# A first sequence in feed-forward units of 128, 256 and 384 tokens in place of three of 256, with a new order of all instructions

## The chip, the core and the metric

The kernel runs on one core of a Trainium2 chip. A core has TensorE (PE in the profile, its weight loads PEld), VectorE (DVE), ScalarE (ACT), GpSimd (POOL) and SyncE (SP), which issues the transfers here. The metric is the device time of one execution in microseconds, and less is better. Times of a comparison are medians of runs on one chip.

## What is computed

Four sequences of 768 tokens go through a linear attention with 8 heads of 48 channels, whose state decays by a complex factor, and then through a feed-forward layer with a short convolution and a gate:

```python
for t in range(S):                     # per sequence and head
    S_re, S_im = ar*S_re - ai*S_im + k[t] v[t]^T, ar*S_im + ai*S_re
    y[t] = q[t] S_re
h = relu(x @ w_in)                     # x: y with heads side by side, 384 channels; w_in 384x1024
conv = sum_k conv_w[k] * h[t + k - 1]  # 3 taps over tokens, zero outside the sequence
out = (h * sigmoid(conv)) @ w_out      # 1024x384
```

## The kernel before

**Attention.** The 24 chunks of 128 tokens (6 for each sequence) are worked through in 12 segments of two. For each segment `a_pre`, `a_log`, `a_trig`, `c_pre` and `c_exp` turn the decay into running logs and angles on ScalarE and VectorE (lines 479 to 577). `c_post` (579) forms the products `qkc_t` (L592), writes them to DRAM (L596) and reads them back in another layout as `stk` (L598). For each chunk `c_chunk` (604) transposes keys on TensorE (L612), copies them (L613), adds to the state (L619) and copies the state (L626). `attention` (656) computes scores (`scores`, L652), multiplies them by a mask on VectorE (L667) in two halves, and multiplies with the values and the state (L676). The result of a chunk is rounded on ScalarE to the high part of `x` (L702), and VectorE makes the low part of it (L703). These two are called the x copy of a chunk here.

**Feed-forward.** It runs over units, each a run of tokens of one sequence (`UNITS`, line 34). A unit's x tiles hold its tokens and one more at each side, since the convolution reaches over the edge. That neighbour column comes out of another unit's x tile by small copies (`halo`, 710, L395). So a unit can start when the chunk behind its last token has its x copy:

```python
UNITS = [[256] * 3, [384] * 2, [384] * 2, [256] * 3]
def need(u):
    b, t0, n = units[u]
    return b * NC + min((t0 + n) // C, NC - 1)
```

A unit takes four steps of two 128-channel blocks each. The front of a step (`moe_front`, 746) is 2 x 9 first-layer matmuls of n + 2 columns into `h_ps` (L758; operands in the type float32r, split in a high and a low part, three products for each of three blocks of channels), the relu on ScalarE (L762) and two passes of the convolution on VectorE (L763, L765). The back (`moe_back`, 768) is the gate's tanh on ScalarE (L420), a product on VectorE (L777), the split of the result into high and low (L783 on ScalarE, L786 on VectorE), and second-layer matmuls of 384 columns into `o` (L793), 2 x 3 for each 128 tokens. After the last step the sums leave by ScalarE (L800) and a transfer (L803). There are two buffers of each x tile and of `h_ps`.

**Order.** The order of the instructions on each engine is written out in a table, `ORDER` (lines 108 to 226): numbers of groups, in program order, for PE, DVE, ACT, POOL and SP. `in_order` (256) chains each engine's instructions in that order and sets ScalarE's table loads (L272) where the next function isn't in the loaded table. So each engine works strictly through its list, and an instruction that waits holds up all that stand behind it on that engine. The weights are loaded and split in the first 80 us, mixed with the rest (L348 to L351, L387 to L390).

Of the kernel before, what the change touches and what calls it, by code (L numbers as in the profile page):

```python
# [33 lines left out]
UNITS = [[256] * 3, [384] * 2, [384] * 2, [256] * 3]  # L34
# [128 lines left out]
    "DVE": [105, 24, 106, 111, 57, 112, 107, 63, 58, 59, 28, 113, 69, 29, 70, 109, 71, 60, 64, 65, 117, 46, 66, 72,  # L163
# [117 lines left out]
def linear_attention_moe_kernel(ctx: ExitStack, tc: tile.TileContext, a, at0, qk, v, w_in, conv_w, w_out, out):  # L281
# [453 lines left out]
    mst = {}  # L735
    units = [(b, sum(UNITS[b][:i]), n) for b in range(B) for i, n in enumerate(UNITS[b])]
    nu = len(units)
# [339 lines left out]
```

## Time and profile before

| | before |
|---|---|
| median of 3 runs | 386.64 us (384.75 to 387.11) |
| profiled execution | 385.09 us, its span 383.3 |
| TensorE busy | 345.3 us, 90% |
| TensorE weight loads busy | 323.5 us, 84% |
| VectorE busy | 337.3 us, 88% |
| ScalarE busy | 333.1 us, 87% |
| mean granted TensorE clock | 0.971 |

The span runs from the first to the last instruction. Busy shares are means over stages with different limits, so the tables by stage say more than the shares. A matmul's length in the trace holds its latency; what it costs in a stream is the distance from its start to the next one's.

### The profile page before, as it was taken

To read this page: it belongs to the slowest core of one execution; us is meant where nothing else is said; L and a number is where in the kernel's file an instruction comes from. 1 tells how busy PE (TensorE), PEld (TensorE's weight loads), DVE (VectorE), ACT (ScalarE), POOL (GpSimd) and SP (SyncE) were. 2 spreads that over 40 slices of the span, in tenths; PEclk is the share of its full clock that TensorE was granted. 3 is DMA by queue.
4 is the path that set the end of the run, shared out by engine and by line. 5 is a ranking of instruction groups with operands and counts; after the bars stand their busy time and mean duration, and the time that the engine had idled before them with its cause. 6 is when DMAs were issued, how large, how long until landed. Compare 5 with 4: busy or idle time off the path is not lost.

```text
span 383.3 us, 12048 instructions
## 1 busy us (share of the span) xinstructions
PE 345.3 (90%) x5220; PEld 323.5 (84%) x5220; DVE 337.3 (88%) x552; ACT 333.1 (87%) x566; POOL 6.9 (2%) x42
## 2 busy tenths in 40 slices
PE   2577277899999999999999999999999999999993
PEld 1566275789999999999998998999999899999993
DVE  3999999989999989999999989898999988567680
ACT  5999999989999999999999998999999965346561
POOL 5000000000000000000000000000000000000000
PEclk9989758999999999999999999999999999999999
DMA  7999989995894957975959566974849828101011
GB/s 285 346 365 345 246 290 254 313 225 198 316 265 165 271 132 292 280 210 235 250 170 289 120 234 264 218 236 167 213 146 301 284 109 213 53 3 65 1 44 50
DMA packets 33423, 81.12 MB, mean 212 GB/s; under 512 B 2128, under 2 KB 23632, under 8 KB 31824
## 3 DMA queue, kind: packets, MB, share of 16 engines
q1 hardware_dynamic: 33360, 80.25, 68.4%
q8 instruction: 43, 0.70, 0.8%
q14 instruction: 20, 0.16, 0.1%
HBM read 56.65 MB, written 23.59 MB: 209 GB/s over the span
## 4 chain that ended last, share of the span: by engine, by line
PE 83%; ACT 7%; DVE 6%; issue 1%; DMA 1%; DVEq 0%
PE h_ps L758 27%; PE o L793 27%; PE ps L676 10%; PE ps L652 9%; PE s_ps L619 4%; PE ps L612 3%; PE o L471 2%; ACT w_t L420 2%; ACT L272 1%; ACT x_t L420 1%; DMA a_t<-in_at 1%; DVE qkc_t L592 1%; ACT w_t L484 1%; DVE p_t L667 1%; DVE x_t L497 0%
## 5 line engine op out<-in xcount | busy, mean ns | idle before, releaser
L793 PE MATMUL o<-wo,hg 128*128 128x384 f32 x576 | 122.3, 342 | 0.5 <-issue 0.4
L758 PE MATMUL h_ps<-x,wi 128*128 128x258 f32 (+1 forms) x720 | 122.4, 308 | 0.0
L758 PEld LDWEIGHTS h_ps<-x,wi 128*128 128x128 f32 x720 | 109.2, 189 | 1.1 <-ACT h_t L762 0.3
L793 PEld LDWEIGHTS o<-wo,hg 128*128 128x128 f32 x576 | 98.6, 188 | 3.1 <-issue 1.1
L272 ACT ACT_TABLE_LOAD x41 | 52.6, 1283 | 0.7
L652 PE MATMUL ps<-stk 96*64 96x128 f32 (+1 forms) x768 | 39.8, 257 | 9.9 <-DMA stk<-qkd 8.2
L652 PEld LDWEIGHTS ps<-stk 96*64 96x64 f32 x768 | 36.0, 142 | 14.8 <-ACT kn L613 10.8
L420 ACT ACTIVATE g_t<-g_t,cw 128x256 f32<-128x256 f32 (+1 forms) x80 | 42.5, 550 | 5.1 <-DVE g_t L765 4.9
L763 DVE SCALAR_TENSOR_TENSOR g_t<-h_t,cw 128x256 f32<-128x256 f32 (+1 forms) x80 | 41.6, 532 | 5.1 <-ACT h_t L762 4.9
L762 ACT ACTIVATE h_t<-h_ps 128x258 f32<-128x258 f32 (+1 forms) x80 | 33.5, 426 | 13.4 <-PE h_ps L758 13.1
L765 DVE SCALAR_TENSOR_TENSOR g_t<-h_t,cw,g_t 128x256 f32<-128x256 f32 (+1 forms) x80 | 41.8, 533 | 1.1
L592 DVE TENSOR_TENSOR qkc_t<-w_t,zz_t 128x1536 f32<-128x1536 f32 x24 | 41.7, 1751 | 0.3
L777 DVE SCALAR_TENSOR_TENSOR g_t<-g_t,h_t 128x512 f32<-128x512 f32 (+1 forms) x40 | 31.6, 791 | 5.7 <-ACT g_t L420 5.6
L786 DVE TENSOR_TENSOR hg<-g_t,hg 128x512 fp32r<-128x512 f32 (+1 forms) x40 | 31.6, 791 | 2.5 <-ACT hg L783 2.4
L783 ACT ACTIVATE hg<-g_t 128x512 fp32r<-128x512 f32 (+1 forms) x40 | 28.5, 716 | 5.9 <-DVE g_t L777 5.5
L667 DVE TENSOR_TENSOR p_t<-ps,mask 128x384 f32<-128x384 f32 x48 | 26.1, 552 | 7.4 <-PE ps L652 6.3
L676 PE MATMUL ps<-p_t,v_t 128*32 128x64 f32 x1344 | 25.7, 223 | 2.6 <-issue 1.7
L676 PEld LDWEIGHTS ps<-p_t,v_t 128*32 128x32 f32 x1344 | 23.0, 112 | 3.7 <-issue 2.2
L676 PE MATMUL ps<-stk,s_sb 96*32 96x128 f32 x640 | 22.1, 275 | 0.6 <-issue 0.4
L612 PE MATMUL ps<-ident,qkc_t 128*128 128x128 f32 x120 | 20.2, 289 | 1.4 <-DMA stk<-qkd 1.1
L484 ACT ACTIVATE w_t<-a_t 128x1536 f32<-128x1536 f32 x12 | 17.9, 1489 | 3.9 <-DMA a_t<-in_at 3.9
L577 DVE TENSOR_TENSOR w_t<-w_t,qk_t 128x1536 f32<-128x1536 f32 x12 | 21.0, 1752 | 0.0
(100 smaller groups left out, 450.8 us busy)
## 6 DMA issues: line engine op xcount, KB each, us to landing
qkd<-qkc_t SPq DMA_DIRECT2D x24, 768.0 KB, 4.2
stk<-qkd SPq DMA_DIRECT2D x24, 768.0 KB, 7.6
v_t<-in_v SPq DMA_DIRECT2D x12, 1024.0 KB, 8.7
qk_t<-in_qk SPq DMA_DIRECT2D x12, 768.0 KB, 6.0
a_t<-in_a SPq DMA_DIRECT2D x10, 768.0 KB, 5.1
out<-os_t SPq DMA_DIRECT2D x24, 192.0 KB, 4.5
hg<-in_w_out SPq DMA_DIRECT2D x8, 384.0 KB, 5.4
h_t<-in_w_in SPq DMA_DIRECT2D x8, 384.0 KB, 4.9
```

The costliest lines, as they stand in the source:

```text
L272: row = [nc.scalar.preload_act_table_set(sets[k]).ins] + row
L420: nc.scalar.activation(out, in_, func=func, **kw)
L592: nc.vector.tensor_tensor(out=qkc, in0=e[:, q:q + 1].broadcast_to([128, 2, NG * w]), in1=zz, op=ALU.mult)
L612: nc.tensor.transpose(tr[:, g - lo], kv[:, g // NG, g % NG], ident)
L652: nc.tensor.matmul(o, lhsT=kt[:, 2 * i + u, part * HC + r:part * HC + r + TM], rhs=qt[:, 2 * i + u, part * HC:C], start=first, stop=part = ...
L676: nc.tensor.matmul(yp[r0:r0 + 32, q // 4, cols], lhsT=left, rhs=right, start=r0 not in started, stop=stop, tile_position=(0, r0), skip_gro ...
L758: nc.tensor.matmul(hp, lhsT=wi[iw][:, f, kt], rhs=x[ix][:, kt], start=(k == 0), stop=(k == 8))
L762: nc.scalar.activation(h, hp, func=AF.Relu)
L763: nc.vector.scalar_tensor_tensor(out=g, in0=h[:, 0:n], scalar=cw[:, f, 0:1], in1=h[:, 1:n + 1], op0=ALU.mult, op1=ALU.add)
L765: nc.vector.scalar_tensor_tensor(out=g, in0=h[:, 2:n + 2], scalar=cw[:, f, 2:3], in1=g, op0=ALU.mult, op1=ALU.add)
L777: nc.vector.scalar_tensor_tensor(out=g, in0=g, scalar=1.0, in1=h[:, :, 1:n + 1], op0=ALU.add, op1=ALU.mult)
L793: nc.tensor.matmul(ops[t][:min(C, n - t * C)], lhsT=hg[:, k, t * C:min((t + 1) * C, n)], rhs=w[:, fw], start=(f == 0 and i == 0), stop=(f ...
```

## The change

The first sequence is cut into units of 128, 256 and 384 tokens. Unit 0 needs chunks 0 and 1 then (before: 0 to 2), unit 1 chunks up to 3 (before: 4), and unit 2 up to 5 as before. The widths of all tiles of these units follow. The other three sequences keep their units. The order of the groups is listed anew for all five engines, with as many groups on each engine as before.

```diff
-UNITS = [[256] * 3, [384] * 2, [384] * 2, [256] * 3]
+UNITS = [[128, 256, 384], [384] * 2, [384] * 2, [256] * 3]
 ORDER = {
-    "PE": [31, 35, 32, 33, 36, 34, 153, 207, 208, 209, 210, 211, 212, 222, 169, 171, 223, 224, 225, 175, 226, 227,
+    "PE": [31, 35, 36, 32, 33, 34, 153, 287, 288, 283, 284, 285, 286, 169, 171, 298, 299, 300, 302, 303, 301, 175,
...
```

What the numbers move is seen in the instructions themselves. On TensorE, behind the last products of chunk 1 (`ps<-p_t,v_t`), there stood before:

```order
L676 MATMUL ps<-stk,s_sb_117 32x128 x16
L612 MATMUL ps<-ident,qkc_t 128x128 x4
L676 MATMUL ps<-p_t,v_t 32x64 x28
L612 MATMUL ps<-ident,qkc_t 128x128 x2
L619 MATMUL s_ps<-v_t,kn 32x48 x24
L612 MATMUL ps<-ident,qkc_t 128x128 x6
L652 MATMUL ps<-stk 64x128
```

And now, with `x_473` and `x_474` the high and low part of unit 0's x:

```order
L676 MATMUL ps<-stk,s_sb_117 32x128 x16
L676 MATMUL ps<-p_t,v_t 32x64 x28
L612 MATMUL ps<-ident,qkc_t 128x128 x6
L758 MATMUL h_ps<-x_473,wi_131 128x130
L758 MATMUL h_ps<-x_474,wi_131 128x130
L758 MATMUL h_ps<-x_473,wi_131 128x130
L758 MATMUL h_ps<-x_474,wi_131 128x130
L758 MATMUL h_ps<-x_473,wi_132 128x130 x2
```

First-layer matmuls begin here, where before the scores of chunk 2 came next; before, the first of them (of 258 columns) stood behind the scores of chunk 3. All 72 of unit 0 stand between this place and the next one.

On TensorE, around the last products of chunk 3, before:

```order
L676 MATMUL ps<-stk,s_sb_119 32x128 x16
L676 MATMUL ps<-p_t,v_t 32x64 x28
L758 MATMUL h_ps<-x_473,wi_131 128x258
L758 MATMUL h_ps<-x_474,wi_131 128x258
L758 MATMUL h_ps<-x_473,wi_132 128x258
```

And now, with `x_546` the x of unit 1:

```order
L676 MATMUL ps<-stk,s_sb_119 32x128 x16
L676 MATMUL ps<-p_t,v_t 32x64 x28
L793 MATMUL o_1228<-wo_133,hg_1232 128x384
L793 MATMUL o_1228<-wo_134,hg_1232 128x384
L612 MATMUL ps<-ident,qkc_t 128x128 x4
L793 MATMUL o_1228<-wo_133,hg_1233 128x384
L793 MATMUL o_1228<-wo_133,hg_1232 128x384
L793 MATMUL o_1228<-wo_134,hg_1232 128x384
L793 MATMUL o_1228<-wo_133,hg_1233 128x384
L612 MATMUL ps<-ident,qkc_t 128x128 x2
L758 MATMUL h_ps<-x_546,wi_131 128x258
L758 MATMUL h_ps<-x_547,wi_131 128x258
```

Before, unit 0 was still in its first layer here (18 of 72 matmuls done). Now its second layer has begun, and the next first-layer matmuls are those of unit 1.

On VectorE, from the second mask product of chunk 2 to that of chunk 3, before (the weights' split, L348 to L390, and the segment steps L485, L546 and L553 are mixed in):

```order
L546 SCALAR_TENSOR_TENSOR zz_t<-reset,x_t 128x768
L703 TENSOR_TENSOR x_762<-ps,x_761 128x3x128
L390 TENSOR_TENSOR wo_134<-hg_293,wo_133 128x384
L485 ISA w_t,gm_126<-w_t 128x768
L485 ISA gm_126 128x1
L667 TENSOR_TENSOR p_t<-ps,mask 128x384
L348 TENSOR_SCALAR hg_309<-hg_308 128x384
L553 SCALAR_TENSOR_TENSOR zz_t<-zz_t 128x768
L349 SCALAR_TENSOR_TENSOR hg_309<-hg_308,hg_309 128x384
L667 TENSOR_TENSOR p_t<-ps,mask 128x384
```

And now the last ten rows of that stretch:

```order
L763 SCALAR_TENSOR_TENSOR g_t<-h_t,cw 128x128
L765 SCALAR_TENSOR_TENSOR g_t<-h_t,cw,g_t 128x128
L553 SCALAR_TENSOR_TENSOR zz_t<-zz_t 128x768
L763 SCALAR_TENSOR_TENSOR g_t<-h_t,cw 128x128
L703 TENSOR_TENSOR x_547<-ps,x_546 128x3x128
L667 TENSOR_TENSOR p_t<-ps,mask 128x384
L763 SCALAR_TENSOR_TENSOR g_t<-h_t,cw 128x128
L348 TENSOR_SCALAR hg_309<-hg_308 128x384
L763 SCALAR_TENSOR_TENSOR g_t<-h_t,cw 128x128
L667 TENSOR_TENSOR p_t<-ps,mask 128x384
```

Convolution passes of unit 0 (L763, L765, 128 columns) stand ahead of and between the mask products of chunk 3, where none stood before.

## Rows read from the trace of the kernel before

**Rows 1.** By stage: length, busy PE, PEld, DVE, ACT, POOL (instructions), granted clock, transfers.

```profile
57.00:82.70 25.70, 20.82 (x506) 18.11 (x503) 24.66 (x42) 23.66 (x37) 0.00 (x0) 0.93 0.98 266
62.00:80.00 18.00, 13.72 (x362) 12.09 (x362) 18.00 (x29) 17.65 (x28) 0.00 (x0) 0.91 0.98 280
80.00:300.00 220.00, 218.41 (x3413) 206.97 (x3407) 208.70 (x309) 215.96 (x363) 1.23 (x12) 1.00 0.76 226
300.00:377.00 77.00, 76.95 (x1044) 74.32 (x1042) 56.38 (x108) 43.69 (x100) 0.21 (x2) 1.00 0.28 89
```

**Rows 2.** Chain that ended last, around the handover: start, length, what.

```profile
70.90 0.48 DVE p_t L667
...
71.42 0.80 PE ps L676 x41
...
80.11 1.51 PE h_ps L758 x11
```

**Rows 3.** The same chain, pieces that give TensorE's prices.

```profile
101.86 1.79 PE ps L676 x88
...
114.21 0.81 PE s_ps L619 x48
115.02 0.81 PE ps L612 x6
...
119.38 2.15 PE h_ps L758 x18
121.53 1.49 PE ps L652 x32
...
194.05 1.24 PE h_ps L758 x7
```

**Rows 4.** Timelines of TensorE and its weight loads: start, length to last end.

```profile
30.75 1.47 PE L471 MATMUL o<-tri,w_t 128*128 128x256 f32 x8
32.05 0.60 PE L471 MATMUL o<-cth,ident 128*128 128x256 f32 x2
...
60.81 0.99 PE L676 MATMUL ps<-p_t,v_t 128*32 128x64 f32 x56
...
81.46 0.60 PE L612 MATMUL ps<-ident,qkc_t 128*128 128x128 f32 x4
...
81.85 0.30 PEld L758 LDWEIGHTS h_ps<-x,wi 128*128 128x128 f32 x2
```

**Rows 5.** Groups by line and form: busy us, mean ns of one | idle before.

```profile
L758 PEld LDWEIGHTS h_ps<-x,wi 128*128 128x128 f32 x720 | 109.2, 189 | 1.1 <-ACT h_t L762 0.3
L612 PE MATMUL ps<-ident,qkc_t 128*128 128x128 f32 x120 | 20.2, 289 | 1.4 <-DMA stk<-qkd 1.1 <-ACT kn L613 0.3
L272 ACT ACT_TABLE_LOAD x41 | 52.6, 1283 | 0.7
L763 DVE SCALAR_TENSOR_TENSOR g_t<-h_t,cw 128x256 f32<-128x256 f32 x48 | 22.4, 479 | 4.0 <-ACT h_t L762 4.0
L763 DVE SCALAR_TENSOR_TENSOR g_t<-h_t,cw 128x384 f32<-128x384 f32 x32 | 19.2, 611 | 1.2 <-ACT h_t L762 0.9
L497 DVE TENSOR_TENSOR x_t<-a_t,x_t 128x768 f32<-128x768 f32 x12 | 11.5, 954 | 1.0 <-ACT x_t L420 0.7
L395 ACT ACTIVATE x<-x 128x3 fp32r<-128x3 f32 x24 | 4.3, 201 | 1.1 <-DVE x L703 1.0
```

**Rows 6.** Timelines of VectorE, and the chain's last piece.

```profile
57.01 0.56 DVE L703 TENSOR_TENSOR x<-ps,x 128x384 fp32r<-128x384 f32 x1 [0.33 <-ACT x L702]
...
76.81 0.55 DVE L667 TENSOR_TENSOR p_t<-ps,mask 128x384 f32<-128x384 f32 x1
...
82.70 0.55 DVE L703 TENSOR_TENSOR x<-ps,x 128x384 fp32r<-128x384 f32 x1
...
84.94 0.88 DVE L763 SCALAR_TENSOR_TENSOR g_t<-h_t,cw 128x256 f32<-128x256 f32 x2
...
368.49 8.47 PE o L793 x48
```

More of the change, by code (lines that the diff above doesn't have):

```diff
@@ L108 @@
 ORDER = {
[54 rows of a table removed]
-    "DVE": [105, 24, 106, 111, 57, 112, 107, 63, 58, 59, 28, 113, 69, 29, 70, 109, 71, 60, 64, 65, 117, 46, 66, 72,
[26 rows of a table removed]
-    "ACT": [23, 26, 27, 25, 30, 108, 152, 114, 199, 202, 38, 41, 37, 43, 203, 40, 206, 42, 156, 154, 201, 159, 161,
[26 rows of a table removed]
-    "POOL": [186, 2, 187, 13, 3, 19, 21, 15, 4, 17, 0, 7, 1, 8, 16, 20, 18, 6, 5, 14, 9, 11, 10, 12, 405, 404, 616,
[7 rows of a table removed]
[54 rows of a table added]
+    "DVE": [57, 24, 58, 105, 59, 106, 111, 63, 107, 112, 28, 60, 46, 113, 69, 29, 64, 70, 109, 65, 71, 117, 47, 61,
[26 rows of a table added]
+    "ACT": [23, 26, 27, 25, 108, 30, 152, 114, 38, 275, 278, 41, 37, 43, 40, 279, 42, 156, 154, 282, 277, 158, 159,
[26 rows of a table added]
+    "POOL": [186, 2, 187, 13, 3, 19, 21, 15, 4, 17, 0, 7, 1, 8, 16, 20, 18, 6, 5, 14, 9, 11, 10, 12, 346, 345, 660,
[7 rows of a table added]
         2052, 2178, 2180, 2234, 2236],
```

220 rows, old and new, of the table ORDER are left out of this document.

## Prediction

> **What bounds the kernel now.** The profiled execution took 385.09 us, with a span of 383.3 and a last matmul that ends at 376.96 [rows 6]; the three timed runs have a median of 386.64, so the profiled one lies 1.55 below it. I read the table by stage first [rows 1]. From 80 us on TensorE is busy in all but 1.6 us of 297 (220.00 less 218.41, and 77.00 less 76.95); VectorE and ScalarE are at 95 and 98% until 300, and at 73 and 57% after. So behind 80 us the kernel ends when TensorE has worked off what is left. From 62 to 80 it is the other way round: VectorE is busy for 18.00 of 18 us and TensorE idles for 4.28. The chain of waits shows the handover [rows 2]: the work that ended last runs on VectorE up to 71.38 (products L592, mask products L667) and on TensorE after it. An edit that lets TensorE do useful work between 62 and 80 shortens the kernel by that work, if VectorE doesn't hand over later for it.
>
> **What is removed, added and moved.** The matmuls of the feed-forward stay in number: 72 first-layer ones (L758) for each unit, 216 for the sequence, and 144 second-layer ones (L793), whose width and count depend on 128-token tiles alone. All other lines keep their counts, but for ScalarE's table loads, 42 before and 40 by the new order. What changes is the widths of the first sequence's units (130, 258 and 386 columns instead of three of 258), when each unit may begin (after chunks 1, 3 and 5 instead of 2, 4 and 5), and the order.
>
> *Price of the first layer.* Eighteen matmuls of 258 columns take 2.15 us, 0.1194 each; seven of 386 take 1.24, 0.177 each [rows 3]. Before: 216 x 0.1194 = 25.8 us. After: 72 x 0.1194 + 72 x 0.177 = 21.3 us and 72 of 130 columns, which the trace doesn't show. Lower bound: the line through the two widths (0.058 for 128 columns) gives 0.062 at 130. Middle: the transposes L612 have the same 128x128 stationary operand and 128 columns; four of them take 0.60 us where one is 0.289 long, so they start 0.104 apart [rows 4, 5]. And where L758 follows them at 81.85, the first of its weight loads has no earlier matmul of its line to hide behind: the second load starts 0.11 after it (two in 0.30, one of them 0.189). So a weight load seems to take about 0.11, which 258 columns (0.119) just cover and 130 don't. Upper bound: plain-f32 matmuls of 128 columns. The L471 group from 30.75 to 32.05 holds eight rows that come from four instructions, two of 256 and two of 128 columns, so each plain-f32 matmul leaves two rows; 1.30 us for 1,536 columns is 0.108 for a row of 128, and 0.22 for a matmul [rows 4]. I take 0.11, since two kinds of rows give it and the operand type is that of L758: 72 x 0.11 = 7.9 us. The bounds give 4.5 and 15.8.
>
> The Trainium skill ("TensorE: Matmul & The Clock Gate", "Back-to-back issue gap") has about 81 ns for a pair of weight load and 128-column matmul in a sustained stream. By it the 72 would take 5.8 us, an estimate; the transposes here take 110 ns, and the row decides.
>
> *Where the 72 lie.* In the new order all of them stand between chunk 1's and chunk 3's last products on TensorE. Chunk 1's end at 61.8 [rows 4]. Other work up to chunk 3's end is 12 transposes (0.81 for six), two state updates (0.81), two score blocks (1.49) and two output products (1.79): 1.6 + 1.6 + 3.0 + 3.6 = 9.8 us [rows 3]. With the 72: 61.8 + 9.8 + 7.9 = 79.5. Before, chunk 3's products ended at 80.11 with only 18 of 258 columns done [rows 2]. So the unit fits into what was idle.
>
> *What VectorE does meanwhile.* From chunk 0's to chunk 3's x copy it works 24.66 of 25.7 us [rows 1]. By the order this stretch gains six L763 and six L765 of 128 columns, L777 and L786 of 256, two L390 and one L497, and loses three L763 and two L765 of 256 columns, one each of L390, L349, L351 and L502, and two small L366. An instruction starts about 0.08 before the one ahead is over (two L763 in 0.88 where one is 0.48) [rows 6], so I count the mean less 0.08: 0.40 for 256 columns, 0.27 for 128 (the line through 0.479 and 0.611 gives 0.347), 0.47 for 384 (a mask product is 0.55 long), 0.87 for L497 [rows 5, 6]. That is 12 x 0.27 + 2 x 0.40 + 0.94 + 0.87 - 5 x 0.40 - 4 x 0.47 - 0.14 = +1.8 us. Without the waits that VectorE had, chunk 3's x copy starts at 57.0 + 24.7 + 1.8 = 83.5 (before: 82.70). Up to chunk 3's second mask product the same count gives +1.9 (three L390 and six narrow ones more, two L349 and the small ones less): 78.7 instead of 76.81 [rows 6]. Its products can end on TensorE about 0.55 + 0.9 later, 80.2.
>
> *The wait that is new.* Behind chunk 3's products the new order has six second-layer matmuls (0.1765 each, 1.06) and six transposes (0.81), then unit 1's first matmuls, which read chunk 3's first column. TensorE reaches them at 82.1. The column is there when the x copy (0.55) and the small copy of the halo (0.20, L395) are done: 83.5 + 0.55 + 0.20 = 84.2 [rows 5, 6]. So about 2 us of waiting from 82.1 to 84.2 take the place of idling near 62 to 80. Queued behind the waiting matmul is everything TensorE has.
>
> *The sum.* Before, 376.96 - 80.11 = 296.85 us lay behind chunk 3's products. Of the first layer 198 matmuls were left (23.6 us), after it 144 (21.3): 2.3 less, whatever the narrow ones cost. The six and six above are 1.9. Left at 84.2: 296.85 - 2.3 - 1.9 = 292.7, so the last matmul ends at 376.9 as before: -0.1 us. The two table loads are 2 x 1.28 us of ScalarE [rows 5], worth at most the 1.6 us that TensorE still waits behind 80; I count 0.3. Together -0.4: 384.7 for the profiled execution's 385.09, and 386.2 against the median of 386.64.
>
> **The rivals.**
> *The unit really fills the idle time (15%).* If the masks and the x copy are not late (VectorE had 1.04 us of slack there, and chunk 1's copy stands earlier in its new order), TensorE alone decides: 79.5 + 1.9 + 292.7 less 1.6 of later waits = 372.5, -4.5: 382.1 against the median. For it: TensorE's 4.28 idle. Against it: VectorE's 18.00 of 18. With the Trainium skill's 81 ns (same page and section) in place of 0.11 this floor would lie 2.1 us lower, an estimate by that page alone.
>
> *Narrow matmuls cost what plain f32 costs (12%), the rival on the other side.* At 0.22 chunk 3's products end at 61.8 + 9.8 + 15.8 = 87.4, and the last matmul at 87.4 + 1.9 + 292.7 = 382.0: +5.0, 391.6. It decides from the price at which TensorE is no longer waiting at 84.2: (84.2 - 1.9 - 61.8 - 9.8) / 72 = 0.149 us. For it: no row of this operand type under 258 columns. Against it: two kinds of rows near 0.11. The granted clock works the same way: it was 0.91 over 62 to 80 [rows 1], part of it at 1.2 GHz, where 0.11 doubles; 3.4 us of that cost about 1.7, which the 2 us wait still covers.
>
> *The new listing suits the chip worse elsewhere (18%).* VectorE's and ScalarE's work ahead of each later chunk's x copy moves by up to 4 us in either direction between chunks 4 and 8 and by about 1 behind them, summed by the new order with the rows' means. If TensorE's 1.6 us of waits behind 80 become three times that, +3.2: 389.8. Against it: the offsets between VectorE's and TensorE's sums shrink by the 3.3 us that TensorE gets more, so TensorE is later at each handover than before, not earlier.
>
> *No change, as summed (55%).*
>
> **How the numbers follow.** About 1% (3.9 us) is what a measurement of this kernel can tell from no change: 382.8 to 390.5. The forecast lies inside. The first rival at 382.1 is faster for most of its chance (0.13); the second is slower (0.12); the third is slower for a third of its chance (0.06). That leaves 0.69 within 1%. The range leaves out the second rival and the far end of the first: 382.3 to 390.6.
>
> **What would show it.** Right: the 130-column matmuls start near 62 us, 0.10 to 0.12 apart; chunk 3's last products end between 79 and 82; a wait of 1 to 2.5 us, released by VectorE's x copy or ScalarE's halo copy, stands just ahead of the first 258-column matmul near 84; from there to the last matmul 292 to 294 us; 40 table loads. Wrong: narrow matmuls 0.15 apart or more; chunk 3's products after 83; or TensorE waits of over 3 us behind 90, which the sum has no place for.

## The result, and the profile after

The changed kernel's 19 executions have a median of 391.54 us (385.49 to 397.31), the kernel before 385.29 (383.49 to 387.11, 19 executions); the ratio is 1.0054, with a 95% interval of 1.0028 to 1.0079. Both numbers are needed to understand the result: eight executions at a mean granted clock of 0.966 to 0.975 took 385.5 to 388.7 us and eleven at 0.938 to 0.962 took 390.2 to 397.3, and the ratio leaves most of the latter out, while none of the 19 of the kernel before passed 387.2. The forecast was 386.2, with 382.3 to 390.6. So it is nearly no change where the clock holds, 0.5% slower, and the median lies 0.9 us above the range because in more than half of the executions the clock doesn't hold.

| | before | after |
|---|---|---|
| profiled execution, its span | 385.09, 383.3 us | 386.46, 384.7 us |
| TensorE busy | 345.3 us | 348.4 us |
| VectorE busy | 337.3 us | 338.7 us |
| ScalarE busy | 333.1 us | 331.3 us |
| mean granted TensorE clock | 0.971 | 0.970 |

The table by stage of the kernel after, which answers to [rows 1] (length, busy PE, PEld, DVE, ACT, POOL with their instructions, granted clock, transfers):

```profile
57.00:82.70 25.70, 23.21 (x457) 20.63 (x449) 24.43 (x43) 24.35 (x43) 0.00 (x0) 0.92 0.92 243
62.00:80.00 18.00, 16.31 (x258) 14.82 (x260) 16.73 (x26) 16.66 (x31) 0.00 (x0) 0.91 0.94 245
80.00:300.00 220.00, 218.11 (x3503) 206.86 (x3502) 210.03 (x309) 213.32 (x353) 1.19 (x12) 1.00 0.76 228
300.00:377.00 77.00, 76.99 (x1044) 74.19 (x1043) 58.97 (x112) 46.35 (x105) 0.20 (x2) 1.00 0.30 94
```

Between 62 and 80 us TensorE went from 13.72 to 16.31 us of work, and VectorE, which had no idle time there before, now has 1.27 us. The unit does fill idle time. But TensorE's timeline shows that it takes longer than what it fills (start, length to the last end, line, shape, count; in brackets the idle time ahead and what ended it, where `issue` means that the engine waited for nothing that the profile shows):

```profile
61.30 0.66 PE L612 MATMUL ps<-ident,qkc_t 128*128 128x128 f32 x4
62.84 0.44 PE L612 MATMUL ps<-ident,qkc_t 128*128 128x128 f32 x2 [0.88 <-DVE x L703]
63.21 1.89 PE L758 MATMUL h_ps<-x,wi 128*128 128x130 f32 x15
65.63 2.12 PE L758 MATMUL h_ps<-x,wi 128*128 128x130 f32 x14 [0.53 <-ACT h_t L762]
...
68.45 1.95 PE L758 MATMUL h_ps<-x,wi 128*128 128x130 f32 x8
...
83.25 0.27 PE L619 MATMUL s_ps<-v_t,kn 128*32 128x48 f32 x2 [1.12 <-issue]
...
84.94 0.97 PE L676 MATMUL ps<-p_t,v_t 128*32 128x64 f32 x56
85.83 0.61 PE L793 MATMUL o<-wo,hg 128*128 128x384 f32 x2
...
87.56 1.68 PE L758 MATMUL h_ps<-x,wi 128*128 128x258 f32 x12
```

Fifteen narrow matmuls in 1.89 us are 0.11 apart, while the eight at 68.45 take 1.95 us: 0.21 apart, at 1.2 GHz. Chunk 3's products end (next start) at 85.83, where the kernel before had 80.11 [rows 2], and the first 258-column matmul starts at 87.56 with no wait of its own. From there on nothing is lost. The chain's last piece, which answers to [rows 6]:

```profile
370.17 8.59 PE o L793 x48
```

It ends at 378.76, 291.2 us behind 87.56, and 1.8 us later than before (376.96).

### The profile page after: what moved, and what is told of

Same layout as the page of the kernel before. It is cut to its first block, busy times and chain, and to the rows that moved or that the text cites. A ratio compares the mean times of both kernels' runs of the same rounds, so it can differ in the third digit from the quotient of the medians.

```text
span 384.7 us, 12047 instructions
## 1 busy us (share of the span) xinstructions
PE 348.4 (91%) x5220; PEld 327.2 (85%) x5220; DVE 338.7 (88%) x552; ACT 331.3 (86%) x564; POOL 6.9 (2%) x42
## 4 chain that ended last, share of the span: by engine, by line
PE 79%; DMA 7%; DVE 6%; ACT 6%; issue 1%; DVEq 0%; ACTq 0%; SPq 0%
PE h_ps L758 27%; PE o L793 26%; PE ps L676 9%; PE ps L652 9%; PE s_ps L619 4%; PE ps L612 4%; DMA a_t<-in_at 3%; DMA stk<-qkd 2%; DMA qkd<-qkc_t 1%; ACT w_t L420 1%; ACT x_t L420 1%; ACT w_t L484 1%; ACT L272 1%; DVE qkc_t L592 1%; DVE x_t L497 0%
## 5 line engine op out<-in xcount | busy, mean ns | idle before, releaser
L758 PE MATMUL h_ps<-x,wi 128*128 128x386 f32 (+2 forms) x720 | 127.6, 315 | 0.9 <-ACT h_t L762 0.7
L793 PE MATMUL o<-wo,hg 128*128 128x384 f32 x576 | 120.2, 341 | 0.2 <-issue 0.2
L758 PEld LDWEIGHTS h_ps<-x,wi 128*128 128x128 f32 x720 | 110.5, 191 | 3.4 <-ACT h_t L762 1.5
L763 DVE SCALAR_TENSOR_TENSOR g_t<-h_t,cw 128x384 f32<-128x384 f32 (+2 forms) x80 | 42.0, 533 | 6.4 <-ACT h_t L762 6.2
L420 ACT ACTIVATE g_t<-g_t,cw 128x384 f32<-128x384 f32 (+2 forms) x80 | 42.1, 548 | 6.1 <-DVE g_t L765 5.9
L765 DVE SCALAR_TENSOR_TENSOR g_t<-h_t,cw,g_t 128x384 f32<-128x384 f32 (+2 forms) x80 | 42.4, 535 | 1.4
L762 ACT ACTIVATE h_t<-h_ps 128x386 f32<-128x386 f32 (+2 forms) x80 | 33.6, 423 | 10.0 <-PE h_ps L758 10.0
L783 ACT ACTIVATE hg<-g_t 128x768 fp32r<-128x768 f32 (+2 forms) x40 | 28.6, 715 | 9.4 <-DVE g_t L777 8.3
L786 DVE TENSOR_TENSOR hg<-g_t,hg 128x768 fp32r<-128x768 f32 (+2 forms) x40 | 31.5, 792 | 4.7 <-ACT hg L783 4.5
L777 DVE SCALAR_TENSOR_TENSOR g_t<-g_t,h_t 128x768 f32<-128x768 f32 (+2 forms) x40 | 31.6, 793 | 3.3 <-ACT g_t L420 3.1
```

Of the source, the lines that this page charges most:

```text
L420: nc.scalar.activation(out, in_, func=func, **kw)
L758: nc.tensor.matmul(hp, lhsT=wi[iw][:, f, kt], rhs=x[ix][:, kt], start=(k == 0), stop=(k == 8))
L762: nc.scalar.activation(h, hp, func=AF.Relu)
L763: nc.vector.scalar_tensor_tensor(out=g, in0=h[:, 0:n], scalar=cw[:, f, 0:1], in1=h[:, 1:n + 1], op0=ALU.mult, op1=ALU.add)
L765: nc.vector.scalar_tensor_tensor(out=g, in0=h[:, 2:n + 2], scalar=cw[:, f, 2:3], in1=g, op0=ALU.mult, op1=ALU.add)
L777: nc.vector.scalar_tensor_tensor(out=g, in0=g, scalar=1.0, in1=h[:, :, 1:n + 1], op0=ALU.add, op1=ALU.mult)
```

## Experiments

Fourteen runs follow, the first of the changed kernel itself and thirteen of edited ones. Times are medians, with the ratio to runs of the kernel before beside them on the same chip. "Changed kernel" is the kernel after; where an edit starts from another, it says so.

### 1. The clock: the same kernel, columns streamed once, twice and half

The first three ask why the time spreads. The changed kernel again, unedited:

> The changed kernel once more, as the yardstick of its three variants on the same chip. Theory A (TensorE time): its runs lie within 1 us of 386.5, 1 to 2 us above the kernel before, because first-layer work of the first sequence costs 72 x (0.112 + 0.1195 + 0.177) in place of 72 x 3 x 0.1195, 3.6 us more on the engine that bounds, and an earlier start gives part of it back. Theory B (clock): some of its runs show a granted clock of 0.95 to 0.96 and 390 to 395 us, the others 0.97 and 386 to 388; the kernel before stays at 0.97 and 384 to 387 in all.

393.05 us (386.82 to 399.56, 13 executions), ratio 1.0039 [1.0001, 1.0077]. Five took 386.8 to 389.3 at clocks of 0.960 to 0.972, eight 392.9 to 399.6 at 0.922 to 0.957; the 23 of the kernel before beside it stay within 384.1 to 389.1. The profile is of an execution of 392.9 us. Its stages:

```profile
62.80:69.40 6.60, 5.16 (x71) 4.32 (x63) 6.60 (x10) 5.97 (x14) 0.00 (x0) 1.00 1.13 234
69.60:86.50 16.90, 16.90 (x217) 15.43 (x218) 10.55 (x17) 10.98 (x19) 0.00 (x0) 0.50 0.59 176
86.70:391.00 304.30, 297.88 (x4565) 283.37 (x4561) 269.38 (x420) 260.52 (x458) 1.40 (x14) 1.00 0.62 189
```

For 16.9 us TensorE was granted 1.2 GHz while it was busy the whole time; in the first profile the same level lasted from 67.95 to 71.25:

```profile
67.95:71.25 3.30, 3.30 (x49) 3.18 (x50) 3.30 (x5) 2.52 (x4) 0.00 (x0) 0.50 0.47 148
```

The first 258-column matmul follows and the chain's last piece ends it:

```profile
93.99 1.26 PE L758 MATMUL h_ps<-x,wi 128*128 128x258 f32 x8
```

```profile
376.91 8.61 PE o L793 x48
```

So 87.56 became 93.99 (+6.4), and the rest is 291.5 us against 291.2. Not all of the 6.4 us lies in that stretch. The x copy of chunk 1, behind which the small unit's matmuls start, came at 62.23 in the first profile and 1.7 us later here (an earlier stretch at 1.2 GHz lasted until 57.7 us there and until 62.7 here):

```profile
62.23 0.55 DVE L703 TENSOR_TENSOR x<-ps,x 128x384 fp32r<-128x384 f32 x1
```

```profile
63.92 0.56 DVE L703 TENSOR_TENSOR x<-ps,x 128x384 fp32r<-128x384 f32 x1
```

From there to the first 258-column matmul it is 4.7 us more, although the issue wait of 1.12 us is missing here: so 5.9 us come from 13.6 us more at half the clock, which are worth 6.8.

Second, each first-layer matmul of the small unit streams its 130 columns twice, into the same bank:

```diff
+            wide = 2 if n == 128 else 1
+            hw = psH.tile([128, 512], F32, name="h_ps")[:, 0:wide * (n + 2)]
+            hp = hw[:, 0:n + 2]
...
-                    nc.tensor.matmul(hp, lhsT=wi[iw][:, f, kt], rhs=x[ix][:, kt],
+                    nc.tensor.matmul(hw, lhsT=wi[iw][:, f, kt], rhs=xs,
```

(`xs` is the same tile broadcast over two copies.)

> Edit: each first-layer matmul of the 128-token unit streams its 130 columns twice (260 columns into the same bank, the second copy is never read). Order, instructions and waits stay. Theory A: a 260-column matmul takes about 0.12 us (as the 258-column ones) against 0.112, so 72 x 0.008 = 0.6 us more, 387. Theory B1 (the lower clock comes with what the narrow matmuls leave undone on the array): no run falls to 0.95-0.96, all within 386 to 389. Theory B2 (the lower clock comes with the new order, not with the narrowness): runs at 0.95-0.96 and 390 to 395 stay as frequent as without the edit.

387.28 us (382.94 to 389.83, 12 executions), ratio 1.0005 [0.9968, 1.0042]; clocks of 0.964 to 0.980, none lower. Twice the columns and 5.8 us less in the median than the changed kernel beside it. The windows show no stretch at 1.2 GHz behind the start, and the group by form what the 72 cost:

```profile
54.90:382.00 327.10, 318.11 (x5005) 300.99 (x4996) 292.50 (x456) 283.67 (x498) 1.40 (x14) 1.00 0.66 196
```

```profile
L765 PE MATMUL h_ps<-x,wi 128*128 128x260 f32 x72 | 11.4, 299 | 0.6 <-ACT h_t L769 0.4 <-ACT x L395 0.2
```

Third, the opposite:

```diff
...
-                    nc.tensor.matmul(hp, lhsT=wi[iw][:, f, kt], rhs=x[ix][:, kt],
+                    nc.tensor.matmul(hp, lhsT=wi[iw][:, f, kt], rhs=x[ix][:, kt, 0:66] if thin else x[ix][:, kt],
...
```

> Edit, the opposite of streaming twice the columns: each first-layer matmul of the 128-token unit streams only 66 of its 130 columns (the other tokens of that unit get the result of the first ones, so half of its output is not computed). Number of matmuls, order and waits stay. If a narrow matmul's price is its weights, it stays at 0.110 to 0.114 us. Theory B1 (what the narrow matmuls leave undone on the array brings the lower clock on): nearly all runs now have a second long stretch at 1.2 GHz behind 60 us, as the one of 69.5 to 86.6 us in the profile of the changed kernel's run of 392.9 us: 392 to 400 us, clock 0.95 or less. Theory B2 (order or chance): as many low-clock runs as without the edit, half of them at 386 to 389.

396.28 us (392.14 to 398.14, 6 executions), ratio 1.0228 [1.0178, 1.0277], clocks of 0.932 to 0.954: all six are long. The windows and the group by form:

```profile
57.70:64.30 6.60, 5.63 (x134) 4.90 (x130) 6.51 (x12) 6.57 (x12) 0.00 (x0) 1.00 1.10 256
64.50:95.00 30.50, 29.93 (x400) 27.85 (x400) 19.64 (x37) 19.30 (x35) 0.21 (x2) 0.50 0.61 179
```

```profile
L759 PE MATMUL h_ps<-x,wi 128*128 128x66 f32 x72 | 15.7, 379 | 0.6 <-ACT h_t L764 0.6
```

30.5 us at 1.2 GHz with TensorE busy for 29.9 of them; half the columns, and 15.7 us of matmuls in place of 11.0. Order and instruction count are the same in all three, so theory B1 holds in this: with the order unchanged, the long stretch goes when each matmul streams more columns and comes in every execution when it streams fewer. The order alone (B2) and chance are out. What the edits changed ahead of the fall is only how many columns each matmul streamed. Idle time there doesn't tell the kernels apart: TensorE was busy for 5.16 of 6.60 us ahead of the 16.9 us above, and for less in a kernel of experiment 3 (48 matmuls that stream their columns twice), whose clock doesn't fall:

```profile
60.50:67.30 6.80, 4.24 (x56) 3.49 (x46) 6.80 (x10) 6.26 (x14) 0.21 (x1) 1.00 1.13 226
```

But narrow matmuls aren't the only way to such a stretch. In the kernel before with dummy matmuls added early (experiment 5) one of 10.2 us holds none of them:

```profile
64.98:75.22 10.24, 9.04 (x179) 8.27 (x182) 9.83 (x10) 9.07 (x12) 0.00 (x0) 0.50 0.96 273
```

### 2. One part alone: the units in the old order

Edit: units of 128, 256 and 384 tokens, with the order lists of the kernel before mapped piece by piece to the new numbers, and an x buffer of its own for the small unit.

> One part of the change alone: units of 128, 256 and 384 tokens, but every engine's order is that of the kernel before (each piece of work in the place that the same piece had; the third token tile of the 384 unit right behind its second; the small unit has an x buffer of its own, without which that order would deadlock). Theory A: nothing starts earlier, so the 3.6 us of TensorE time come in full: chunk 3's products near 80, as before, and 389 to 391 us at 0.97 clock. Theory that the new listing, not the units, costs the time: 386 to 387 here. Theory B2: no low-clock runs here; theory B1: low-clock runs here too, since 72 narrow matmuls remain.

391.82 us, ratio 1.0124 [1.0085, 1.0163]: 4.8 us (3.3 to 6.3), which takes in the 3.6 expected. Theory A holds and the rival that the listing costs the time falls: the new listing gives back some 2.7 us of it (1.0124 less 1.0054), by putting the small unit into the idle time. One of the six executions is long (399.0 at a clock of 0.943), so the low clock is met in this order too; in the new order 19 of 32 took 390.2 us or more, and six executions can't say whether the order has a part in that.

### 3. Does TensorE bound 61 to 87 us?

From the kernel with the columns streamed twice, three times instead:

```diff
-            wide = 2 if n == 128 else 1
+            wide = 3 if n == 128 else 1
```

> Edit: the 128-token unit's 130 columns are streamed three times (390 columns, copies never read) in place of twice; number of instructions, order and waits stay, and neither a lower clock nor another length of TensorE's stream comes in. The 386-column matmuls take 0.177 us against 0.12. Theory A (TensorE bounds from 61 us to 87 us, and all of it reaches the end): 72 x 0.057 = 4.1 us more than with the columns streamed twice: first 258-column matmul near 91.4, 391 us. Rival (the narrow matmuls fill idle time beside VectorE and ScalarE): less than 1 us of it, 387 to 388.5.

389.44 us (387.31 to 391.01), ratio 1.0113 [1.0076, 1.0150], against 1.0005 for twice: 2 us by the medians' distance to the kernel before, 4 by the ratios. The group by form gives the added work, the timeline what arrived:

```profile
L765 PE MATMUL h_ps<-x,wi 128*128 128x390 f32 x72 | 15.4, 356 | 0.4 <-ACT h_t L769 0.4
```

```profile
89.22 2.28 PE L765 MATMUL h_ps<-x,wi 128*128 128x258 f32 x17
```

15.4 less 11.4 is the 4.0 us expected. The first 258-column matmul comes at 89.22 in place of 87.35: 1.9 of the 4.0. But the kernel that streams twice lost 1.44 us in this stretch to an issue wait, which the kernel that streams three times lacks. The waits of the former, up to 87.35 us:

```profile
PE s_ps L619 <- issue: 1.4, 1, 1.4
PE ps L612 <- DVE x L703: 0.6, 1, 0.6
PE h_ps L765 <- ACT h_t L769: 0.4, 1, 0.4
```

The x copies of chunk 1 start within 0.1 us of each other (62.34 and 62.24), so 3.2 of the 4.0 us arrive: theory A, not the rival, for work that is added.

Taking work away was harder. The small unit leaves out one of its three terms, 24 of 72 matmuls:

```diff
-                for iw, ix in ((0, 0), (0, 1), (1, 0)):
+                for iw, ix in (((0, 0), (1, 0)) if n == 128 else ((0, 0), (0, 1), (1, 0))):
...
```

> Edit: the 128-token unit leaves out its 24 matmuls of the low half of x against the high half of the weights (48 narrow ones in place of 72; this low-order term is missing in the output of that unit). Theory A: TensorE bounds between 61 and 86 us, so 24 x 0.112 = 2.7 us less: chunk 3's products end near 83 in place of 85.8, time 383.8 at the 0.97 clock. Rival (VectorE and ScalarE bound that stretch, the narrow matmuls fill idle time): less than 0.7 us less. Theory B has no opinion on the size, but expects low-clock runs to become rarer.

398.78 us (394.07 to 401.13), ratio 1.0275 [1.0212, 1.0338]: 13 us slower than the kernel before, with less work. No theory expected that. The first 258-column matmul starts at 87.44, nearly as in the changed kernel, but the last matmul ends at 390.7, 303.3 us behind it in place of 291.2. TensorE's waits there, its timeline at the longest, and the transfers of 179.0 to 182.2 us:

```profile
PE ps L676 <- issue: 4.4, 3, 3.0
PE ps L652 <- issue: 2.3, 1, 2.3
PE s_ps L619 <- issue: 2.1, 1, 2.1
```

```profile
178.49 0.66 PE L676 MATMUL ps<-p_t,v_t 128*32 128x64 f32 x27
182.16 1.07 PE L676 MATMUL ps<-p_t,v_t 128*32 128x64 f32 x29 [3.02 <-issue]
```

```profile
q8 instruction: 1, 0.02, 1.9%
```

TensorE stops in the middle of 56 small products, in which nothing is waited for that the profile shows, and one block of instructions arrives meanwhile. Four such waits make 8.5 of the 12.1 us, and two stretches of 3.4 us at 1.2 GHz that follow on two of them (from 181.9 and 222.9 us) up to 3.4 more. Theory C: leaving 24 matmuls and their weight loads out shifts where the blocks of TensorE's instructions end, everywhere behind. The next kernel was to undo that by filling the early wait:

> Edit: as the kernel with 48 in place of 72 narrow matmuls (the same low-order term is missing in the output), and 24 matmuls of one column into a spare bank in TensorE's wait ahead of chunk 0's scores, so that TensorE's instruction stream behind them has its old length. That kernel lost 12 us behind 134 us, in four TensorE waits of 1.1 to 3.0 us that the profile puts to issue (8.5 us), each beside a 16 KB transfer of the instruction queue, and two 3.4 us stretches at 1.2 GHz (3.4 us). Theory C (where the stream's 16 KB blocks end against the dense runs of small matmuls): with the old length these waits go, and the time falls to 383 to 387 at a clock near 0.97. Theory that leaving out the 24 matmuls itself upsets the later order: 394 to 401 stays.

391.32 us (388.13 to 394.10). Most of the 12 us is gone, but not all: a plain-f32 matmul leaves two rows, so the stream was now 24 matmuls too long (5,244 rows for 5,220) and one wait of 2.0 us stood at 112. The profile is of an execution with 17 us at 1.2 GHz, so it can't tell about the bound. The same with the columns streamed twice:

> Edit: 48 in place of 72 narrow matmuls (the low-order term of x is missing in that unit's output), each streaming its columns twice, and 24 matmuls of one column in the wait ahead of chunk 0's scores, which keep TensorE's instruction stream at its old length. With the clock and the stream's length out of play, what is left is 24 matmuls less. Theory A (TensorE bounds from 61 us on): 24 x 0.12 = 2.9 us less than the wide ones alone, the first 258-column matmul near 84.5 in place of 87.35 us, 384.4 us, faster than the kernel before by 1 us. Rival (VectorE, ScalarE and the transfers bound that stretch): less than 0.7 us of it, 386.6 or more.

391.31 us, ratio 1.0152. Chunk 3's products end 1.7 us earlier than with all 72, but issue waits of 2.4 us at 86 and 1.8 us at 110 follow, so the run is inconclusive for theory A. Two more have the filling right, 12 matmuls in place of 24:

> As the kernel with 48 matmuls whose columns are streamed twice (the low-order term of x is missing in that unit's output), but with 12 in place of 24 plain-f32 matmuls of one column in the early wait: each leaves two rows in the profile, so 24 made TensorE's stream 24 matmul rows longer than the changed kernel's (5244 for 5220), and 12 make it equal behind the small unit. Theory A (TensorE bounds from 61 to 87 us): chunk 3's products near 83, first 258-column matmul near 84.5 in place of 87.35, and 384.4 us, 2.9 less than with all 72. Theory C (where the stream's blocks end): the waits of 2.4 us at 86 and 1.8 us at 110 that the 24 brought are gone. Rival to A: 386.6 or more without such waits.

385.19 us (383.67 to 386.57, 12 executions), ratio 0.9995 [0.9971, 1.0018]. The timeline and the chain's last piece:

```profile
84.65 1.53 PE L771 MATMUL h_ps<-x,wi 128*128 128x258 f32 x10
```

```profile
367.76 8.65 PE o L806 x48
```

The first 258-column matmul starts at 84.65 (expected 84.5, with all 72 at 87.35), and the last matmul ends at 376.4 in place of 378.7: 2.7 us earlier at the hand-over and 2.3 at the end of the profile; by the ratios of timed runs the difference (0.1%) is within the intervals, by the medians' distance to the kernel before it is 1.7 us. The 2.7 look like the 2.9 of theory A, but 1.4 of them is the issue wait that the kernel with all 72 had and this one hasn't. And TensorE's waits up to 84.65 us for the relu on ScalarE (`h_t`) and for VectorE's x copy have grown, from 0.4 and 0.6 us with all 72:

```profile
PE h_ps L771 <- ACT h_t L775: 1.7, 3, 0.9
PE ps L618 <- DVE x L709: 1.2, 1, 1.2
```

With the x copy of chunk 1 at 62.15 in place of 62.24, the 24 matmuls themselves bring 1.2 of 2.9 us. The kernel with 48 and no filling agrees: from its x copy (63.67) to 87.44 it is, without the changed kernel's issue wait, 0.4 us shorter for the 2.7 expected. So TensorE bounds the stretch in one direction: work that is added to it arrives for the most part, and of work that is taken away more than half comes back as waits for ScalarE and VectorE, as the rival said. Each of these comparisons is one profile against another. The two issue waits at 86 and 110 are gone.

> The same with the 130 columns streamed once (48 matmuls; the same term is missing in the output). Theory C: TensorE's stream is as long as the changed kernel's behind the small unit (5220 matmul rows), so none of the waits of 2 to 3 us behind 134 us that cost the kernel with 48 and no filling 12 us. Theory B1: the granted clock still falls for long in about half of the runs: 384 to 386 without it, 390 to 396 with it.

388.19 us (386.87 to 392.07). The profile is of an execution of 392.1 us, at 1.2 GHz from 67.6 to 88.1, and from its first 258-column matmul (92.20) to the end (384.7) it takes 292.5 us: the 303.3 of the first kernel without the 24 are gone, and with them its 2 to 3 us waits. This pair, whose only difference is 12 matmuls of one column in a wait from 40 us on, bears theory C out. B1's lower times (384 to 386) did not come: seven of eight executions lie at 386.9 to 390.1.

### 4. Do the changes between kinds of matmul cost it?

Edit: on TensorE the 72 stand in four runs among the attention of chunks 2 and 3, in place of eight.

> Edit: on TensorE alone, the 72 narrow matmuls stand in 4 runs among the attention of chunks 2 and 3 in place of 8; nothing else moves. Theory (each change between narrow matmuls and attention pieces costs TensorE about 0.25 us: 0.20 ahead of the first and 0.166 in place of 0.111 behind it): 4 x 0.25 = 1 us less, the first 258-column matmul near 86.5 in place of 87.56 us, 385.5 to 386.5 at a clock near 0.97. Theory B1 on the clock: it still falls for long in about half of the runs (390 and more), or in more, since longer runs of narrow matmuls stand alone. Rival (the pieces held back make VectorE and ScalarE late): first 258-column matmul at 87.5 or later.

390.43 us (388.11 to 391.39), ratio 1.0124; at 1.2 GHz for 3.4 and 10.2 us behind 59 us, and the first 258-column matmul at 91.1. The expected 1 us did not come.

> Both edits: 4 runs in place of 8, and the 130 columns streamed twice. Theory: no second low-clock stretch behind 60 us, and 1 us less than with the wide ones alone: 385.5 to 386.5, no more than 0.3% from the kernel before. Rival: as with the wide ones alone, 387.3.

387.97 us, ratio 1.0062 [1.0033, 1.0091], not better than the eight runs. TensorE's waits between 60 and 95 us, and the 72:

```profile
PE ps L658 <- DVE x L709: 2.1, 1, 2.1
PE ps L658 <- ACT kn L619: 1.3, 1, 1.3
```

```profile
L771 PE MATMUL h_ps<-x,wi 128*128 128x260 f32 x72 | 10.1, 292 | 0.1
```

The 72 do get cheaper by 1.3 us (11.4 to 10.1), but 3.4 us of waits for VectorE and ScalarE stand where the narrow ones had been woven in, and the first 258-column matmul starts at 87.56. My theory falls, its rival holds: the interleaving pays for itself.

### 5. Can the start be had back?

Edit: 18 matmuls on constants in TensorE's wait ahead of chunk 0's scores, on the kernel with the columns streamed twice and on the kernel before.

> Edit: the 128-token unit's columns streamed twice, and 18 matmuls of 128x256 on constants into a spare bank in TensorE's wait ahead of chunk 0's scores (41 to 51 us; results never read), which keep the engine busy there. In the profile with the columns streamed twice TensorE runs at 1.2 GHz from 44.5 to 54.8 us, because it has been waiting, and does chunk 0 and part of chunk 1 at that level. Theory (TensorE bounds from 51 us on, clock included): chunk 0's scores and products at 2.4 GHz save about half of the 51 to 54.8 us stretch, 1.5 to 3 us in all: 384 to 385.5, below the kernel before. Rival (DMA, ScalarE and VectorE hold the start up to 62 us): same as without the dummies, 386.5 to 388. Rival against: the dummies end after the awaited transfer, 1 us slower.

392.07 us, ratio 1.0158. The clock is at 2.4 GHz from 41 to 59 us, but chunk 1's products end at 63.2 in place of 61.7, since waits for VectorE and ScalarE of 2.0, 1.6 and 0.8 us stand between. And an issue wait of 3.1 us at 85.6 and one of 3.5 at 110.8 follow: the dummies moved the stream.

> Edit on the kernel before: the same 18 matmuls in the wait ahead of chunk 0's scores (40.8 to 49.05 us there). Theory: chunk 0 and 1 run at 2.4 GHz, but VectorE bounds 62 to 80 us, so at most 1 us is left of it: 384.5 to 386. If TensorE bounded the kernel before from 49 us on as well: 382.5 to 384.

390.05 us, ratio 1.0097 [1.0064, 1.0130]. No gain at 62 us either (chunk 1's products at 62.8 for 61.8), and an issue wait of 3.6 us at 298. Up to 62 us the rival (transfers, ScalarE and VectorE hold the start) is right for both; the times, with issue waits of 3.6 and 6.6 us in them, can't say more. No kernel that computes everything beat the kernel before.

## Why the prediction was wrong, step by step

Two steps failed. The sum of TensorE's work up to chunk 3 was too small, which by itself left the time 0.5% longer; and the term for the clock, put at 1.7 us and covered, took the median out of the range.

- *Price of a narrow matmul: right.* 0.11 was said, 0.109 to 0.115 is the distance of starts within a run at 2.4 GHz, far from both bounds, 0.062 and 0.22. At 66 columns it stays 0.111, so the columns don't set it. (The 110 ns that the prediction names for the transposes is 0.104 by its own rows; the sum doesn't use it.)
- *Start: right.* Chunk 1's products end at 61.4 (61.8 said).
- *"Where the 72 lie", TensorE alone at 79.5: the first step that failed.* It took each piece at its price in a stream without a wait or a change, at full clock. The stretch from chunk 1's to chunk 3's products took 24.5 us where 17.7 was said. The 72 cost 11.0 in place of 7.9 (waits for h_t 0.7, eight at 1.2 GHz 0.8, the rest at the seven places where they resume behind attention pieces), the other pieces 13.5 in place of 9.8, 2.0 of it the waits of 0.88 and 1.12 us and some 0.7 the 1.2 GHz. In the one other arrangement that was tried (experiment 4) this was no slack to be planned away: what is saved at the changes comes back as waits for two engines that are nearly as full.
- *VectorE sets chunk 3's products: wrong with it.* The second mask product starts at 80.80 (78.7 said) and the x copy at 86.50 (83.5 said). The copy waits for ScalarE's, and that one for TensorE's products, so VectorE follows here and doesn't lead. It and ScalarE lie close behind, though: experiment 3 meets them as soon as TensorE has less to do. The rows of VectorE answer to [rows 6], the third is ScalarE's:

```profile
80.80 0.56 DVE L667 TENSOR_TENSOR p_t<-ps,mask 128x384 f32<-128x384 f32 x1
...
86.50 0.56 DVE L703 TENSOR_TENSOR x<-ps,x 128x384 fp32r<-128x384 f32 x1 [1.08 <-ACT x L702]
```

```profile
85.97 0.49 ACT L702 ACTIVATE x<-ps 128x384 fp32r<-128x384 f32 x1 [1.10 <-PE ps L676]
```

- *"The wait that is new", 2 us: wrong.* There is none ahead of the first 258-column matmul. It was to be the cover for the low clock ("which the 2 us wait still covers"), so with it went the cover.
- *What is left behind: right.* 292.7 us said, 291.2 measured; 40 table loads said, and 39 of one line and one of another are there:

```profile
L272 ACT ACT_TABLE_LOAD x39 | 50.0, 1283 | 0.6
```

- *Sum where the clock holds:* 3.4 late at the hand-over (87.56 for 84.2), 1.5 better behind it (some 0.9 of that because TensorE idles there for 0.8 us in place of 1.6): +1.9, 0.5%. That is within 1%, as forecast, but as two errors that offset each other in part and not as the sum had it.
- *The clock: the step that took the time out of the range.* The prediction gave it "3.4 us of that cost about 1.7", covered by a wait. In the profile of 386.5 us it was 3.4 us indeed, with no wait to cover them; in that of 392.9 us it was 17 us, and the 13.6 us more cost 5.9 us up to the hand-over; with 66 columns it was 30.7 us, and with 260 or 390 none (experiments 1 and 3). The range had no room for it: I read the granted clock of the kernel before as given, although the change puts another kind of matmul exactly where that clock was low. Why fewer columns keep the clock low, and why only in more than half of the executions, stays open.
- *The rival on the other side* came out in its effect, TensorE no longer waiting at 84.2, and not in its cause. By its measure the 72 took 11.04 / 72 = 0.153 us each, above its threshold of 0.149, but with waits and clock counted in; a matmul by itself stayed at 0.11, and the threshold goes by 9.8 us for the other pieces, which took 13.5.

## What to carry to other kernels

The columns streamed count twice: a matmul of this type cost 0.11 us with 66 columns as with 130, little less than the 0.119 with 258, and a stretch of the narrow ones can also lose half the clock, so a unit that is split narrower for an earlier start should first be priced with both. A sum of one engine's work is a floor, not a time, where two other engines are over 90% full in the same stretch. And an edit that adds or drops instructions on TensorE can bring waits far behind it, 8.5 us of them here; compare variants of equal instruction count, or look at the issue waits before a difference is believed.

## What the runs showed of the hardware

Columns and clock: with 66, 130, 260 and 390 columns in each of the same 72 matmuls, the stretch at 1.2 GHz behind 60 us was 30.7, 3.4 or 17, none, and none; the granted clock was 0.50 while TensorE was busy for 16.90 of 16.90 us and 29.93 of 30.50. The Trainium skill ("TensorE: Matmul & The Clock Gate", "HAM oscillation — how this bites in real kernels") explains a clock that falls in the middle of a kernel by gaps in which the engine idles; here 1.4 us of idle time lie in the 6.6 us ahead of the fall, but the clock then stayed low on an engine without gaps, and in the kernel with 48 wide ones it didn't fall behind 2.6 us of idle time in 6.8, so the measurement goes beyond that page.

Instruction blocks: the instruction queue moves 43 blocks, 0.70 MB in all, and TensorE has thirteen waits of 1.1 to 3.6 us that end by "issue" in these traces (behind 40 us), nine of them in runs of small attention matmuls. In each of the thirteen it goes on 1.25 to 1.58 us after a block has landed, whatever the wait's length. That the block is what is waited for is inferred from this and from the pair of experiment 3. The Trainium skill ("Runtime: NRT & Kernel Launch", "Instruction fetch mechanics") says that the cost of crossing a block's border is "mostly hidden"; mostly is right for the kernel before (its longest such wait is 0.9 us), and not for the kernel without the 24 matmuls, which lost 8.5 us in four of them.
